# Chunks 1 and 2 of a windowed attention with one softmax group each, and the next projection in front of the down products

## The chip, the cores and the metric

The kernel runs on one core of one Trainium2 chip. The metric is the device time of one execution in microseconds, lower is better. Before the change it was 259.79 us, the median of three runs (259.69 to 259.99).

A core has engines that run side by side, each with its own queue of instructions in order: TensorE (PE in the profile; PEld is its weight load), VectorE (DVE), ScalarE (ACT), GpSimd (POOL) and SyncE (SP), whose queue here only issues DMAs. ACT and POOL issue DMAs too. Semaphores order work between engines.

## What is computed

A layer norm, a windowed attention with 32 heads of 20 elements, in which each position attends to itself and the seven positions 2, 4, ... 14 before it, and a gated bilinear block beside it; both are added to x.

```python
x = A_x                                   # 1 x 2048 x 640
xn = _layernorm(x, axis=-1)
return x + _A_ref(xn, A_wqkv, A_wo) + _B_ref(xn, B_w_gate, B_w_up, B_w_down)
# A: W, dil = 8, 2
logits = jnp.einsum("bhsd,bhswd->bhsw", q, kg) * scale
attn = _softmax(logits, axis=-1)
o = jnp.einsum("bhsw,bhswd->bhsd", attn, vg)      # then o @ wo
# B: F = 1536
g = jnp.einsum("bsd,df->bsf", x, w_gate)
u = jnp.einsum("bsd,df->bsf", x, w_up)
return jnp.einsum("bsf,fd->bsd", g * u, w_down)
```

## The kernel before

The 2048 rows are 16 tiles of 128 (`t`), in four chunks of 512 (`c`, four tiles `q` each). All arithmetic on features works on transposed activations: `xnT` holds the normed rows of a chunk with features on partitions.

For each chunk there are these steps.

- **LN** (`ln`, L344, for chunks 0 and 1 on DVE; `ln_chunk`, L315, for chunks 2 and 3 on ACT: two passes for mean and square, one that applies them). The x tiles are loaded by DMA into five buffers. `LN_HOLD` (L299) names, for each tile of chunks 2 and 3, the step after which its first ACT pass may begin. An entry of two numbers names a hidden block `HT[c, f]`, one of three numbers an eviction of the projection, `R[r, c][j]`.
- **Transposes** (`transposes`, L369): from tile 4 on by transposing DMAs on SP's queue into `xnT`, which has `XB` buffers: two, or three when `EARLY` is set.
- **Projection** (`proj`, L487): 75 matmuls of 512 columns, 25 each for query, key and value, evicted by ACT (L498). `project(c)` also copies the 14 rows of halo for keys and values.
- **Products** (`products` and `fold`, L522 to L567): DVE multiplies the query with the shifted keys of two positions of the window at a time, for one half of the chunk's rows, 2560 elements per instruction, into `pw`, and folds the five feature groups together; the last fold of each pair writes over the first part of the keys' or the queries' buffer.
- **Logits** (`logits`, L569): PE sums those over the 4 partitions of a head with the matrix `Ek` (128 x 32), into `lps`, tag `pl`. Before, each chunk has two groups `g`, one per half of the rows. Each is 8 matmuls of 256 columns in column tiles of 32, four side by side, in one of two `pl` buffers of one PSUM bank.
- **Softmax** (`softmax`, L595), per group: DVE maximum and subtract, ACT exponential (L620), DVE sum, reciprocal and multiply into `a`.
- **Round trip** (`store` and `spread`, L638 to L649): each head's weights are needed on all of its partitions. SP's queue stores `a` (128 KB) to a DRAM tile `aD`, and loads it back with each row repeated on four partitions, as `aE` (512 KB).
- **Value products** (`av`, L661): per tile DVE multiplies the shifted values by `aE`, in two instructions of 2560 elements (L674), and adds the eight window positions in three steps (L684, L682) to `oT`.
- **Gated products** (`glu`, L708): 12 hidden blocks `f`, for each 5 matmuls with `wg` and 5 with `wu` (L717), evicted by ACT to `gs` and `us` (L722) and multiplied by DVE to `hT` (L734).
- **Down** (`down`, L769): per tile and half of the output columns, 12 matmuls with `hT` and `wd` (L783) and 5 with `oT` and `wo` (L786), into one bank, evicted by ACT to `y` (L798). POOL's queue adds `y` to the output by an accumulating DMA (L827), onto x, which was copied there by DMA beforehand (`seed`); the last two tiles are added on DVE and stored by SP. For the first tile of a chunk the ten first hidden blocks and `oT` go first, and the last two blocks follow.

The order in each queue is not written out but planned when the kernel is built. Each step is an `add(engine, cost, fn, deps, occ=...)`; `Plan.order` (L60) walks a model of the engines, takes the step that is ready and whose due time is earliest, and emits the instructions in that order. Due times come from the chain of costs behind a step. `margin` is added in front of a follower, `PACE` scales all costs of an engine, `urgent` puts a step first, and `kb` adds a model of a DMA queue. PE's main work (`pe_main`) is one chain in the order in which the steps are added; the logits are not in this chain and may be put between any two of its steps. So the planned costs move no work by themselves, they decide the order only.

The order of PE's chain is set by the loop at the end (L905 on): attention and gated products of chunk c, LN of chunk c+2, then the four down steps of chunk c, and then the projection of chunk c+2; with `EARLY` the projection comes in front of the down steps.

Of the kernel before, what the change touches and what calls it, by code (L numbers as in the profile page):

```python
# [9 lines left out]
ACT = mybir.ActivationFunctionType  # L10
ALU = mybir.AluOpType
# [21 lines left out]
class Plan:  # L33
# [1 line left out]

    LAG = 0.06
    RAW = 0.116
    PACE = {"DVE": 1.03, "ACT": 1.0}
    INORDER = ("DVE", "PE", "ACT")

    def __init__(self):
# [70 lines left out]
def kernel(  # L112
# [11 lines left out]
    nc = tc.nc  # L124
# [171 lines left out]
    def apply_in(t):  # L296
        XT[t] = inline("DVE", 0.443, ln_apply(t), [RS[t]], 0.4)

    LN_HOLD = ((0,2),(0,3),(0,4),(0,5),(1,2),(1,3),(1,4),(1,5))  # L299

    def held(at):
        return HT[at] if len(at) == 2 else R[at[0], at[1]][at[2]]
# [59 lines left out]
        return main  # L362

    XDMA = 4
    EARLY = False
    XB = 3 if EARLY else 2
    GP = {}

# [58 lines left out]
            X[t + 5] = add("POOL", 6.0, load_x(t + 5, nc.gpsimd), [a], occ=0.45, kb=160)  # L427

    LL = {}
    PV = {}  # L430
    R = {}
    PROJ = ("q", "k", "v")
# [2 lines left out]
    def halo(c, r):  # L435
        def fn():
            k = new((PROJ[r], c), [P, KT, HALO + CS], BF, PROJ[r], 2)
            if c == 0:
                nc.gpsimd.memset(k[:, :, 0:HALO], 0.0)
            else:  # L440
                nc.scalar.copy(k[:, :, 0:HALO], T[PROJ[r], c - 1][:, :, CS : CS + HALO])
        if c == 0:
            HALOCP[r, c] = add("POOL", 0.3, fn, after=[RS[0]])
        else:
            w = LL.get(2 * c - 3) if r == 1 else O16.get(CH * (c - 1) - 1)
            HALOCP[r, c] = add("ACT", 0.25, fn, [w, *R[r, c - 1]])

    def lhs(r, i, j):
# [38 lines left out]
    def proj(c, r, lo=0, n=CS):  # L487
        for j in range(KT):
            key = ("qkv", c, r, j, lo)

            def pe(key=key, j=j):
                new(key, [P, 512], F32, "ps", 6, psum)
                for i in range(KT):
                    nc.tensor.matmul(T[key][:, 0:n], lhsT=lhs(r, i, j),  # L494
                                     rhs=T["xnT", c][:, i, lo : lo + n], start=(i == 0), stop=(i == KT - 1))

            def ev(key=key, j=j):
                nc.scalar.copy(where(r, c, j, j + 1, lo, n)[:, 0, :], T[key][:, 0:n])  # L498

            ts = range(c * CH + lo // P, c * CH + (lo + n) // P)  # L500
            old = LL.get(2 * c - 3) if r < 2 else O16.get(CH * (c - 1) - 1)
            a = pe_main(KT * (n / 2400 + 0.0027), pe, [*WW[r], *[TT[t] for t in ts], *[TX.get(t) for t in ts], old])
            e = add("ACT", 0.16 + n / 1200, ev, [a, HALOCP.get((r, c)), R.get((r, c - 2), [None])[0]], occ=0.07 + n / 1200)
            ring.append(e)
            R.setdefault((r, c), []).append(e)
# [37 lines left out]
    def products(c, hf):  # L543
        for j in range(4):
            i = 4 * hf + j
            u = i // 2

            def mul(u=u, j=j):
                if j % 2 == 0:
                    new(("pw", c, u), [P, 4, KT, HS], BF, *(("av", 2) if c == 0 and hf else ("pw", 2)))  # L550
                o = T["pw", c, u][:, 2 * (j % 2) : 2 * (j % 2) + 2, :, :]
                lo = hf * HS
                qh = T["q", c][:, :, lo : lo + HS]
                kh = T["k", c][:, :, lo + DIL * 2 * j : lo + DIL * 2 * j + HS]
                qh = bass.AP(tensor=qh.tensor, offset=qh.offset, ap=[list(qh.ap[0]), [0, 2], *[list(x) for x in qh.ap[1:]]])
                kh = bass.AP(tensor=kh.tensor, offset=kh.offset, ap=[list(kh.ap[0]), [DIL, 2], *[list(x) for x in kh.ap[1:]]])
                nc.vector.tensor_tensor(o, qh, kh, ALU.mult)  # L557

            m = 8 * c + i
            w = None if c == 0 else LL[0] if c == 1 and hf == 0 and FIRST < 3 else FO[4 * c + u - 2]  # L560
            PW[m] = add("DVE", 1.48, mul, [*R[0, c], *R[1, c], w], occ=1.395, after=[PW.get(m - 1)])
        for u in (2 * hf, 2 * hf + 1):
            FO[4 * c + u] = fold(c, u)

    PAIRED = ()

    E = HS // 4  # L567

    def logits(c, g):  # L569
        n = 2 * c + g  # L570

        def lg():
            l = new(("lps", n), [P, W, E], F32, "pl", 2, psum)
            parts = [summed(c, 2 * g + b) for b in range(2)]
            last = len(parts[0]) - 1
            for i in range(last + 1):
                for b in range(2):
                    for j in range(4):
                        nc.tensor.matmul(l[H * j : H * (j + 1), 4 * b : 4 * b + 4, :], lhsT=Ek[:],  # L579
                                         rhs=parts[b][i][:, :, E * j : E * (j + 1)],  # L580
                                         start=(i == 0 and b == 0), stop=(i == last), tile_position=(0, H * j), skip_group_check=True)

        alone = not (g and c in PAIRED)
        took = 0.022 + 0.2195 * (len(LEFT) if c == 0 else 1) + (0.19 if alone else 0.0)
        LL[n] = add("PE", took + 0.13, lg, [FO[2 * n], FO[2 * n + 1], FO[4 * c + 3] if c in PAIRED else None, LL.get(n - 1), AA.get(n - 2), CE], occ=took)
        LL[n].urgent = True
        LL[n].margin = (0.9 if c == 0 else 2) if alone else 0.0

    def prodlog(c):
        for g in range(2):  # L590
            products(c, g)
        for g in range(2):
            logits(c, g)

    def softmax(c, hf):  # L595
        n = 2 * c + hf

        def small(op, occ, deps):
            return add("DVE", occ + 0.083, op, deps, occ=occ)

        def mask():
            ps = T["lps", n]
            nc.vector.tensor_tensor(ps[0:H, :, 0:HALO], ps[0:H, :, 0:HALO], negm[0:H], ALU.add)

        def top():
            m = new(("m", n), [P, E], F32, "m", 1)
            nc.vector.tensor_reduce(m[:], T["lps", n][:].rearrange("p w s -> p s w"), AX.X, ALU.max)

        def sub():
            d = T["d", n] = T["lps", n]  # L610
            nc.vector.tensor_tensor(d[:], d[:], T["m", n][:, None, :].to_broadcast([P, W, E]), ALU.subtract)

        a = LL[n]
        if n == 0:
            a = small(mask, 0.18, [a, CM])
        a = small(top, 0.6, [a])
        DD[n] = small(sub, 0.609, [a, AA.get(n - 1)])

        def ex():
            nc.scalar.activation(T["d", n][:], T["d", n][:], ACT.Exp, scale=scale)  # L620

        e = add("ACT", 0.635, ex, [DD[n]], occ=0.54)
        e.margin = 0.8

        def total():
            s = new(("s", n), [P, E], F32, "s", 1)
            nc.vector.tensor_reduce(s[:], T["d", n][:].rearrange("p w s -> p s w"), AX.X, ALU.add)

        def rec():
            nc.vector.reciprocal(T["s", n][:], T["s", n][:])  # L630

        def scaled():
            a = new(("a", n), [P, W, E], BF, "a", 1)
            nc.vector.tensor_tensor(a[:], T["d", n][:], T["s", n][:, None, :].to_broadcast([P, W, E]), ALU.mult)

        AA[n] = small(scaled, 0.609, [small(rec, 0.47, [small(total, 0.6, [e])]), AS.get(n - 1)])

        def store():  # L638
            aD = new(("aD", n), [H, 4, W * E], BF, "aD", 2, dram)
            nc.sync.dma_start(out=aD[:].rearrange("h e f -> e h f"), in_=T["a", n][:].rearrange("p w s -> p (w s)"))  # L640

        def spread():
            ae = new(("aE", n), [P, 4, W, E], BF, "aE", 2)
            src = T["aD", n][:]
            src = bass.AP(tensor=src.tensor, offset=src.offset, ap=[[4 * W * E, H], [0, JL], [1, 4 * W * E]])
            nc.sync.dma_start(out=ae[:], in_=src)

        AS[n] = add("SP", 3.3, store, [AA[n], AE.get(n - 2)], occ=0.5, kb=128)
        AE[n] = add("SP", 3.9, spread, [AS[n], AM.get(2 * n - 3)], occ=0.5, kb=512)  # L649

    BY_DMA = ()
    AS = {}
# [6 lines left out]
        WL["o"] = SPLAST[0] = add("SP", 8, wo_load, after=[SPLAST[0]], occ=0.5, kb=800)  # L659

    def av(t):  # L661
        n, u = divmod(t, 2)
        c, q = divmod(t, CH)

        def mul(b):
            def fn():
                if b == 0:
                    new(("av", t), [P, W, KT, P], BF, "av", 2)
                o = T["av", t][:, :, :, b * E : (b + 1) * E]
                w = T["aE", n][:, 2 * u + b, :, :]  # L670
                w = bass.AP(tensor=w.tensor, offset=w.offset, ap=[list(w.ap[0]), [E, W], [0, KT], [1, E]])
                v = T["v", c][:, :, q * P + b * E : q * P + b * E + E]
                v = bass.AP(tensor=v.tensor, offset=v.offset, ap=[list(v.ap[0]), [DIL, W], *[list(x) for x in v.ap[1:]]])
# [10 lines left out]
                    nc.vector.tensor_tensor(v[:, 0:k], v[:, 0:k], v[:, k : 2 * k], ALU.add)  # L684
            return fn

        w = LL[1] if t < 2 else O16.get(t - 2)
        a = add("DVE", 1.48, mul(0), [AE[n], w, *R[2, c]], occ=1.40, after=[O16.get(t - 1) if ONE else AM.get(t - 1)])
        a = AM[t] = add("DVE", 1.48, mul(1), [AE[n]], occ=1.40, after=[a])
        def tree_dma(k):  # L690
            def fn():
                v = T["av", t]
# [193 lines left out]
    def attention(c):  # L886
        prodlog(c)
        if c == 0:
            SPLAST[0] = WL["u"]
            load_down()  # L890
            load_out()
        for hf in range(2):
            softmax(c, hf)
        for q in range(CH):
            av(c * CH + q)

# [58 lines left out]
```

## Time and profile before

| | |
|---|---|
| median of 3 runs | 259.79 us |
| the profiled execution's own time | 258.83 us |
| its span, first to last instruction | 256.9 us |
| PE busy | 251.4 us (98%) |
| DVE busy | 226.2 us (88%) |
| ACT busy | 129.1 us (50%) |
| granted TensorE clock | 0.999 |
| `aE` spread, 512 KB, issue to landing | 3.4 to 4.8 us, median 3.6 |
| `y` store, 160 KB, issue to landing | 3.6 us, median |
| idle time of DVE before value products, for `aE` | 8.9 us in 3 waits |

In the lines of the profile, L is the line of the kernel, the text after it names what is written and read, and xN counts instructions. In the chain of waits in order of time, the columns are start, length and what held the chain; in the timeline, start, length, engine, line and operation, and in brackets how long the engine had been idle and for whom. The matmuls' ends are modelled, so neighbouring matmuls overlap in the timeline by about 0.16 us and the chain counts by ends. The sums by stage give, after the stretch, its length, the busy time and number of instructions of PE, PEld, DVE, ACT and POOL, the granted clock, the share of the DMA engines and their rate.

### The profile page before, as it was taken

The page shows a single profiled execution, that of the slowest core. Times are in us where ns is not written, and L with a number is a line of the kernel's source. Part 1 is how long each engine was busy: PE and PEld are TensorE (multiplying, and loading weights), DVE is VectorE, ACT ScalarE, POOL GpSimd, SP SyncE. Part 2 cuts the span into 40 slices and gives each one's busy share as a digit, 9 for nine tenths or more (in the row PEclk, how much of TensorE's full clock was granted, in tenths as well). Part 3 has the DMA queues.
Part 4 walks back from the last instruction along what each step waited for, and adds up shares of the span by engine and source line. Part 5 has one row for each costly group of instructions (what it writes and reads, how often), then busy time and mean ns, then how long its engine had stood idle before and what let it go on. Part 6 is the DMA issues. An engine that isn't in the chain of part 4 may idle for free.

```text
span 256.9 us, 3821 instructions
## 1 busy us (share of the span) xinstructions
PE 251.4 (98%) x1493; PEld 140.3 (55%) x1493; DVE 226.2 (88%) x299; ACT 129.1 (50%) x251; POOL 33.9 (13%) x59
## 2 busy tenths in 40 slices
PE   6999999999999999999999999999999999999995
PEld 2955554444677555444477655444457654445762
DVE  5679999999999998999999964999999975999911
ACT  2756555798551364689662254655531233754100
POOL 2530000002142100003702110000301210000110
PEclk9999999999999999999999999999999999999999
DMA  7989996102165402032327232020022243020221
GB/s 224 346 200 239 397 374 225 69 23 82 25 117 95 46 12 93 0 102 102 106 52 98 32 46 82 7 97 0 27 79 26 26 61 94 20 82 3 26 26 52
DMA packets 19969, 24.48 MB, mean 95 GB/s; under 512 B 9104, under 2 KB 17296, under 8 KB 19888
## 3 DMA queue, kind: packets, MB, share of 16 engines
q1 hardware_dynamic: 16608, 17.70, 22.2%
q0 software_dynamic: 2384, 5.41, 12.4%
q10 hardware_dynamic: 960, 1.15, 1.3%
q8 instruction: 11, 0.18, 0.3%
q14 instruction: 6, 0.05, 0.1%
HBM read 18.61 MB, written 5.96 MB: 96 GB/s over the span
## 4 chain that ended last, share of the span: by engine, by line
PE 96%; DVE 1%; DMA 1%; ACT 0%; issue 0%
PE ps L717 40%; PE ps L494 23%; PE ps L783 20%; PE ps L786 8%; PE ps L468 2%; PE pl L579 1%; DMA x<-in_A_x_dram 1%; DVE st L252 1%; PE ps L393 0%; ACT xnT L399 0%; DVE x L271 0%; DVE x L794 0%; DVE mv L258 0%; DVE ve L260 0%
## 5 line engine op out<-in xcount | busy, mean ns | idle before, releaser
L717 PE MATMUL ps<-xnT,wu 128*128 128x512 bf16 x240 | 59.7, 379 | 0.0
L717 PE MATMUL ps<-xnT,wg 128*128 128x512 bf16 x240 | 59.6, 379 | 0.0
L783 PE MATMUL ps<-wd,hT 128*128 128x320 bf16 (+2 forms) x384 | 57.4, 299 | 0.0
L674 DVE TENSOR_TENSOR av<-v,aE 128x2560 bf16<-128x2560 bf16 x32 | 47.6, 1486 | 8.9 <-DMA aE<-aD 8.9
L783 PEld LDWEIGHTS <-hT 128*128 128x128 bf16 x384 | 37.0, 98 | 16.1 <-issue 0.4
L557 DVE TENSOR_TENSOR pw<-q,k 128x2560 bf16<-128x2560 bf16 x28 | 40.6, 1486 | 0.9 <-ACT k L498 0.9
L717 PEld LDWEIGHTS <-wg 128*128 128x128 bf16 x240 | 23.5, 98 | 28.1
L717 PEld LDWEIGHTS <-wu 128*128 128x128 bf16 x240 | 23.3, 98 | 28.3 <-issue 0.4
L684 DVE TENSOR_TENSOR av<-av 128x2560 bf16<-128x2560 bf16 (+1 forms) x32 | 36.9, 1154 | 0.3
L722 ACT CAST us<-ps 128x512 bf16<-128x512 f32 x48 | 28.2, 587 | 17.3 <-PE ps L717 17.3
L722 ACT CAST gs<-ps 128x512 bf16<-128x512 f32 x48 | 28.1, 586 | 16.7 <-PE ps L717 16.7
L798 ACT COPY y<-ps 128x320 f32<-128x320 f32 x28 | 11.7, 426 | 45.5 <-PE ps L786 30.7
L786 PE MATMUL ps<-wo,oT 128*128 128x320 bf16 (+2 forms) x160 | 27.0, 299 | 0.0
L528 DVE TENSOR_TENSOR pw<-pw 128x2048 bf16<-128x2048 bf16 (+1 forms) x28 | 25.2, 952 | 0.0
L827 POOL DMA_DIRECT2D out_dram<-y x14 | 12.3, 876 | 82.1 <-ACT y L798 81.6
L494 PE MATMUL ps<-xnT,wk 128*128 128x512 bf16 x100 | 22.6, 380 | 0.0
L734 DVE TENSOR_TENSOR hT<-gs,us 128x512 bf16<-128x512 bf16 x48 | 20.2, 420 | 2.6 <-ACT us L722 2.4
L494 PE MATMUL ps<-xnT,wv 128*128 128x512 bf16 x100 | 22.4, 379 | 0.0
L786 PEld LDWEIGHTS <-oT 128*128 128x128 bf16 x160 | 15.5, 98 | 6.3
L498 ACT CAST k<-ps 128x512 bf16<-128x512 f32 x20 | 11.7, 586 | 11.0 <-PE ps L494 11.0
L494 PEld LDWEIGHTS <-wv 128*128 128x128 bf16 x100 | 11.7, 118 | 9.9 <-issue 0.2
L494 PE MATMUL ps<-xnT,wq 128*128 128x512 bf16 x75 | 16.9, 379 | 0.0
(69 smaller groups left out, 197.0 us busy)
## 6 DMA issues: line engine op xcount, KB each, us to landing
aE<-aD SPq DMA_DIRECT2D x8, 512.0 KB, 3.6
out_dram<-y POOLq DMA_DIRECT2D x14, 160.0 KB, 3.6
out_dram<-in_A_x_dram POOLq DMA_DIRECT2D x3, 640.0 KB, 4.3
wg<-in_B_w_gate_dram SPq DMA_DIRECT2D x1, 1920.0 KB
wu<-in_B_w_up_dram SPq DMA_DIRECT2D x1, 1920.0 KB, 12.7
wd<-in_B_w_down_dram SPq DMA_DIRECT2D x1, 1920.0 KB
x<-in_A_x_dram SPq DMA_DIRECT2D x11, 160.0 KB, 6.4
aD<-a SPq DMA_DIRECT2D x8, 128.0 KB
```

The costliest lines, as they stand in the source:

```text
L494: nc.tensor.matmul(T[key][:, 0:n], lhsT=lhs(r, i, j), rhs=T["xnT", c][:, i, lo : lo + n], start=(i == 0), stop=(i == KT - 1))
L498: nc.scalar.copy(where(r, c, j, j + 1, lo, n)[:, 0, :], T[key][:, 0:n])
L528: nc.vector.tensor_tensor(w[:, :, lo:hi, :], w[:, :, lo:hi, :], w[:, :, a:b, :], ALU.add)
L557: nc.vector.tensor_tensor(o, qh, kh, ALU.mult)
L674: nc.vector.tensor_tensor(o, v, w, ALU.mult)
L684: nc.vector.tensor_tensor(v[:, 0:k], v[:, 0:k], v[:, k : 2 * k], ALU.add)
L717: nc.tensor.matmul(ps[:], lhsT=(wu if r else wg)[:, i, f * P : (f + 1) * P], rhs=T["xnT", c][:, i, :], start=(i == 0), stop=(i == KT - 1))
L722: nc.scalar.copy(s[:], T[key][:])
L734: nc.vector.tensor_tensor(h[:], T["gs", c, f][:], T["us", c, f][:], ALU.mult)
L783: nc.tensor.matmul(ps, lhsT=T["hT", c, f][:, q * P : (q + 1) * P], rhs=wd[:, f, sl], start=(f == 0), stop=(f == FT - 1 and not wo_part))
L786: nc.tensor.matmul(ps, lhsT=T["oT", t][:, g, :], rhs=wo[:, g, sl], start=False, stop=(g == KT - 1 and f1 == FT))
L827: nc.gpsimd.dma_start(out=out_flat[t * P : (t + 1) * P, :], in_=T["y", t][:], accum_op=ALU.add)
```

## The change

Four things are changed together. `GR` gives the number of logits and softmax groups of each chunk: two for chunks 0 and 3, one for chunks 1 and 2. A chunk's groups now share one `pl` tile of two PSUM banks, one `a`, one `aE` (1 MB, one buffer instead of two of 512 KB). In chunks 1 and 2 a group is 8 matmuls of 512 columns, each softmax instruction has twice the elements, one store and one spread carry 256 KB and 1 MB, and a value product is one instruction of 5120 elements per tile. `EARLY` is set, with a third `xnT` buffer. The planned costs of store and spread are 3.6 and 4.2 instead of 3.3 and 3.9, without the model of a queue, `PACE` of DVE is 1.01 instead of 1.03, and `LN_HOLD` lets the LN passes of chunk 2 begin at the projection of chunk 1.

```diff
-    PACE = {"DVE": 1.03, "ACT": 1.0}
+    PACE = {"DVE": 1.01, "ACT": 1.0}
-    LN_HOLD = ((0,2),(0,3),(0,4),(0,5),(1,2),(1,3),(1,4),(1,5))
+    LN_HOLD = ((1,1,0),(2,1,0),(2,1,2),(2,1,4),(0,11),(0,11),(0,11),(0,11))
-    EARLY = False
+    EARLY = True
     XB = 3 if EARLY else 2
+    GR = (2, 1, 1, 2)
...
     def logits(c, g):
-        n = 2 * c + g
+        n = (c, g)
+        E = CS // 4 // GR[c]
         def lg():
-            l = new(("lps", n), [P, W, E], F32, "pl", 2, psum)
-            parts = [summed(c, 2 * g + b) for b in range(2)]
+            if g == 0:
+                new(("lps", c), [P, 2 * CS], F32, "pl", 1, psum)
+            l = T["lps", c][:, g * W * E : (g + 1) * W * E].rearrange("p (w s) -> p w s", w=W)
...
-                        nc.tensor.matmul(l[H * j : H * (j + 1), 4 * b : 4 * b + 4, :], lhsT=Ek[:],
-                                         rhs=parts[b][i][:, :, E * j : E * (j + 1)],
-                                         start=(i == 0 and b == 0), stop=(i == last), tile_position=(0, H * j), skip_group_check=True)
+                        at = g * 4 * E + j * E
+                        rhs = summed(c, 2 * (at // HS) + b)[i][:, :, at % HS : at % HS + E]
+                        first = i == 0 and (b == 0 or GR[c] == 1)
+                        nc.tensor.matmul(l[H * j : H * (j + 1), 4 * b : 4 * b + 4, :], lhsT=Ek[:], rhs=rhs, start=first,
+                                         stop=(i == steps - 1), tile_position=(0, H * j), skip_group_check=True)
-        LL[n].margin = (0.9 if c == 0 else 2) if alone else 0.0
+        LL[n].margin = 0.9 if c == 0 else 1.5
...
-            aD = new(("aD", n), [H, 4, W * E], BF, "aD", 2, dram)
-            nc.sync.dma_start(out=aD[:].rearrange("h e f -> e h f"), in_=T["a", n][:].rearrange("p w s -> p (w s)"))
+            if g == 0:
+                new(("aD", c), [GR[c], H, 4, W * E], BF, f"aD{GR[c]}", 2, dram)
+            nc.sync.dma_start(out=T["aD", c][g].rearrange("h e f -> e h f"), in_=T["a", c][:, g * W * E : (g + 1) * W * E])
...
-            ae = new(("aE", n), [P, 4, W, E], BF, "aE", 2)
-            src = T["aD", n][:]
+            if g == 0:
+                new(("aE", c), [P, 4 * W * P], BF, "aE", 1)
+            src = T["aD", c][g]
...
-        AS[n] = add("SP", 3.3, store, [AA[n], AE.get(n - 2)], occ=0.5, kb=128)
-        AE[n] = add("SP", 3.9, spread, [AS[n], AM.get(2 * n - 3)], occ=0.5, kb=512)
+        AS[n] = add("SP", 3.6, store, [AA[n], AE.get((c - 2, GR[c - 2] - 1))], occ=0.5)
+        AE[n] = add("SP", 4.2, spread, [AS[n], AM.get(CH * c - 1)], occ=0.5)
...
     def av(t):
-        n, u = divmod(t, 2)
         c, q = divmod(t, CH)
+        E = CS // 4 // GR[c]
+        parts = P // E
...
-        a = add("DVE", 1.48, mul(0), [AE[n], w, *R[2, c]], occ=1.40, after=[O16.get(t - 1) if ONE else AM.get(t - 1)])
-        a = AM[t] = add("DVE", 1.48, mul(1), [AE[n]], occ=1.40, after=[a])
+        for b in range(parts):
+            w = 0.065 + 2.67 / parts
+            a = add("DVE", w + 0.085, mul(b), [ae, LL[0, GR[0] - 1] if t < 2 else O16.get(t - 2), *R[2, c]], occ=w,
+                    after=[a or (O16.get(t - 1) if ONE else AM.get(t - 1))])
+        AM[t] = a
```

The softmax's instructions take the slice of their group in the shared tiles `pl`, `m`, `s` and `a`. In the loop at the end nothing else is changed:

```python
        if EARLY and c + 2 < NCH:
            project(c + 2)
        for q in range(CH):
            down(c * CH + q)
        if not EARLY and c + 2 < NCH:
            project(c + 2)
```

## The prediction

> **What bounds the kernel now.** I read the page first (busy time and the chain of waits), then the chain in order of time, then sums by stage, then the queue of SP and the timeline of DVE around the DRAM round trip of the softmax.
>
> ```profile
> span 256.9 us, 3821 instructions
> PE 251.4 (98%) x1493; PEld 140.3 (55%) x1493; DVE 226.2 (88%) x299; ACT 129.1 (50%) x251; POOL 33.9 (13%) x59
> PE 96%; DVE 1%; DMA 1%; ACT 0%; issue 0%
> ```
>
> PE is never let go: the chain is PE from 5.64 us to 253.78 us. So a change gains only what it takes off PE's own stream, and costs what it makes PE wait.
>
> ```profile
> 85.55 2.16 PE ps L494 x10
> 87.71 0.33 PE pl L579 x8
> 88.04 13.08 PE ps L494 x60
> 101.12 0.33 PE pl L579 x8
> 101.45 1.21 PE ps L494 x5
> ...
> 164.12 25.90 PE ps L717 x120
> 190.02 1.36 PE ps L783 x10
> 191.38 0.68 PE ps L786 x5
> 192.06 1.36 PE ps L783 x10
> 193.42 0.68 PE ps L786 x5
> 194.10 2.17 PE ps L783 x16
> ```
>
> Two logits groups (pl) lie in the projection of chunk 2; after the gated products of chunk 2 (to 190.02), down 8 takes its first ten hidden blocks and the attention product, and at 194.10 needs the last two blocks of hT. Stage sums price a group:
>
> ```profile
> 85.55:102.66 17.11, 17.11 (x93) 8.85 (x91) 16.32 (x18) 9.27 (x17) 0.86 (x1) 1.00 0.22 49
> 102.66:128.56 25.90, 25.90 (x123) 11.78 (x121) 25.35 (x33) 19.86 (x41) 7.36 (x7) 1.00 0.23 77
> 128.56:147.47 18.91, 18.91 (x146) 13.36 (x144) 18.56 (x21) 7.36 (x14) 2.69 (x3) 1.00 0.44 62
> 147.47:164.12 16.65, 16.65 (x85) 8.81 (x83) 11.24 (x14) 9.03 (x16) 0.86 (x1) 1.00 0.22 49
> ```
>
> The first number after each stretch is its length; PE and DVE busy are the first and third with a count. The two projections differ by one group: 17.11 - 16.65 = 0.46 us. DVE is as full as PE (16.32 of 17.11, 25.35 of 25.90, 18.56 of 18.91): it is the engine that could become the bound. What it waits for:
>
> ```profile
> 143.17 0.86 POOL L827 DMA_DIRECT2D out_dram<-y  x1 [3.73 <-ACT y L798]
> 148.23 0.86 POOL L827 DMA_DIRECT2D out_dram<-y  x1 [4.20 <-ACT y L798]
> 148.70 0.54 SPq L640 DMA_DIRECT2D aD<-a  x1
> 153.97 0.55 SPq L646 DMA_DIRECT2D aE<-aD  x1
> 157.48 1.49 DVE L674 TENSOR_TENSOR av<-v,aE 128x2560 bf16<-128x2560 bf16 x1 [5.28 <-DMA aE<-aD]
> 165.17 0.55 SPq L640 DMA_DIRECT2D aD<-a  x1
> 168.47 0.54 SPq L646 DMA_DIRECT2D aE<-aD  x1
> 193.01 0.42 DVE L734 TENSOR_TENSOR hT<-gs,us 128x512 bf16<-128x512 bf16 x1
> ```
>
> Store aD to spread aE is 3.3 us at 165.17, but 5.27 where a y store was issued 0.5 us earlier (148.23). DVE lost 5.28 us there, and its last hT of chunk 2 ended at 193.43, half a microsecond ahead of PE's need: DVE's queue was nearly the bound already.
>
> **The change, part by part.**
>
> *Logits, PE.* 120 matmuls of 512 columns take 25.90, so 0.216 each, and 256 columns stream in 0.108. A group streams 2 x 0.108 (four column tiles run side by side); the rest of its cost, 0.44 to 0.46 by stage, is about 0.235 for entering and leaving the form. One group of 512 columns: 0.235 + 2 x 0.216 = 0.667. Before, chunk 1 pays 0.46 + 0.46 and chunk 2 pays 18.91 - 18.47 (down 0, no group) = 0.44, plus 0.46. Saved: 0.92 + 0.90 - 2 x 0.667 = 0.49 us. No row has such a 512-column group: at most it costs what two cost (saves 0), at least what one of 256 does (saves 0.9); the streaming row puts it at 0.49.
>
> *Softmax and value products, DVE.* Each saves fixed time per instruction: 10 softmax instructions and 8 value products fewer. From 2560 and 1280 elements (1.486 and 0.822) an element costs 0.52 ns, so 5120 take 2.82 and hold the queue 2.74, against 2 x 1.40. Like the softmax rows this is off the path as long as DVE meets PE's needs, below.
>
> *Projection c+2 in front of down c; LN of c+2 earlier.* The same matmuls in another order: 0 on PE in itself. What it needs moves with it. ACT's LN passes of chunk 2 (8 statistics passes of 0.93 to 1.03 with their accumulator reads, 4 of 0.92) now lie from the projection of chunk 1 on; ACT is busy 21.1 of the 36 us from 5 to 41, and its order puts them between evictions, so the evictions stay ahead of PE. On POOL three x loads go out before the first y store instead of between y stores; on SP the eight transposes (1.25 us of issue each) go ahead of chunk 1's aD, not around it. With the third xnT buffer they no longer wait for the last gated product. By the same walk as below the last transpose of chunk 2 lands at 62.8, PE wants it at 67.1; chunk 3's at 101.3 for 128.3. So I cost them at nothing; the cover is 4 us of gated products, and if it were gone PE would wait one for one in front of the projection. The two planned costs and PACE change order alone, and that order is what I walk.
>
> *One pl tile, three waits.* Chunk 0's second group now waits for the first group's exponent sums (same tile). In DVE's order one product and two folds stand in front; following DVE's row times the sums end 0.1 us before PE comes. Cost 0; bounds 0 and 0.6, the wait if ACT's exponential (0.59) came one eviction later. The merged groups wait for all four folds instead of two; these end 3 us ahead of PE.
>
> *Round trip.* Between 93.9 and 101.2 us aD moves at a flat 95 GB/s and aE near 400. Doubling adds 131 KB / 95 = 1.38 and 524 KB / 400 = 1.31: aD 3.3 + 1.35 = 4.65, aE 3.6 (page median) + 1.35 = 4.95; with 0.07 of hand-overs R = 9.65 from the end of the scaled attention to the first value product. Bounds: nothing added, 7.0; the whole transfer phases added (1.8 and 2.05, slow starts too), 10.8.
>
> *Does PE then wait?* DVE's order after the change, walked at row pitches. Anchor: hT 1 of chunk 1 waits for ACT; chunk 1's first starts at 105.48 before, the next pair is 2.16 later, minus 0.25 saved by then: 107.39. From there to the start of chunk 2's last hT: 22 hT x 0.335 = 7.4; 18 of 2560 x 1.40 = 25.2; 8 of 5120 x 2.735 = 21.9; 5 of 2048 x 1.135 = 5.7; 12 of 1024 x 0.60 = 7.2; 7 of 1280 x 0.74 = 5.2; 6 oT x 0.40 = 2.4; one double softmax 5.5; top and subtract of chunk 3's first group 1.2; 17 dependent starts x 0.12 = 2.0. Sum 83.8. PE's need is 194.10 - 0.49 + 0.44 (chunk 3's first group now comes before it) less 0.16 of the chain's offset and 0.15 for hand-over and weight load, less the 0.42 of hT and plus 0.14 as it is the second block: 193.45. So DVE may wait 193.45 - 107.39 - 83.8 = 2.26 us in all. It waits twice, R less the work it has between (8.5 in chunk 1 as in chunk 2: folds, three products, hT): 2 x (9.65 - 8.5) = 2.3. That is 0.05 over: the stall in down 8 is 2 x (R - 9.63). Taken 0.1, bounds 0 (R up to 9.6) and 2.3 (R = 10.8). Behind the late hT queue down 8 to 11 and all later PE work; nothing later gives it back.
>
> Sum: 258.83 for the profiled execution (span 256.9 + 1.93 around it) - 0.49 + 0.1 = 258.4. The runs' median is 0.96 above that execution; the same change on it gives 259.4.
>
> **Rivals.**
>
> *A. A y store cuts into the doubled aD of chunk 2 (slower).* The last y store of down 7 follows its stage by 0.76 (147.47, 148.23). After: 128.31 + 16.2 + 19.1 = 163.6, so 164.4, with its packets 1.4 later (as at 148.23) at 165.8. aD of chunk 2 goes out at 162.3 by the same walk and moves packets until about 166.5. For: the trace's collisions cost 5.27 - 3.3 = 2.0 and, at 210.31, 4.82 - 3.6 = 1.2. Against: there the y store came first; here aD does, and the transfer that starts first seems to be served first. It decides from the moment aD is still moving at 165.8. Price 1.2 to 2.0 with no slack left: 259.4 + 1.5 = 260.9. The Trainium skill (DMA: Bandwidth & Descriptors, Queues, rings and completion order) says each engine alternates between queues after whole packets of some 9 to 17 descriptors; by that rule the y store does get in between, or just misses. No row here shows that order.
>
> *B. Transfers slower than their steady rate (slower).* R = 10.8 or part of it: stall up to 2.3, so 260.2 to 261.7. For: aE landings vary from 3.4 to 4.8 at one size. Against: clean aD are all 3.3.
>
> *C. More is gained (faster).* If the unprofiled runs, 0.96 longer than the profile, now hold stalls where the last hT has 0.5 us of cover, the projection in front removes some: 259.4 - 0.6 = 258.8. For: that thin cover. Against: the runs agree within 0.3.
>
> *D. The change does not do what it says:* PE's order, read from the built program, does show the merged groups and the moved projections, so no chance is given.
>
> **How the numbers follow.** Forecast 0.45, A 0.22, B 0.20, C 0.13. What a measurement can tell from no change is 0.2%, 0.52 us, so 259.27 is the border of faster: the forecast lies just inside, and 0.12 of its 0.45 beyond. Faster 0.12 + 0.13 = 0.25; same 0.33 + 0.04 of A + 0.03 of B = 0.40; slower 0.35. Range: from 258.9, inside C, to 261.6, the end of B; the forecast's own is 259.2 to 259.8.
>
> **What would show it.** Right: 8 instead of 16 logits matmuls in chunks 1 and 2 and about 0.67 for each group; DVE waiting 1.0 to 1.3 for aE before both first value products; PE without a gap at down 8. A: an aD of chunk 2 of 6 us and a gap in PE near 194. B: both aE landings above 5.4. The prediction is wrong if PE waits anywhere else, above all at the logits of chunk 0 or 3, or in a projection for xnT.

## The result, and the profile after

The changed kernel takes 261.1 us (median of 12 runs, 260.55 to 264.11) where the kernel before takes 259.92 (median of 12 on the same chip, 259.17 to 260.16). The ratio is 1.0076, 95% interval 1.0056 to 1.0096: slower by 0.8%. The two medians alone are 0.45% apart; the ratio also weighs the four of the 12 runs that lie at 262.8 us or more. The ratios in this document leave out runs more than 1.5% above the fastest of their kernel, two of ten in the two-store kernel and one of six in the last one. Forecast were 259.4 us and no change; 261.1 lies in the stated range, 258.9 to 261.6, near its upper end. The profiled execution took 260.83 us against 258.83.

The page of the changed kernel: instructions and span, busy time, and the shares of the chain of waits.

```profile
span 259.1 us, 3747 instructions
...
PE 250.5 (97%) x1459; PEld 140.2 (54%) x1477; DVE 225.3 (87%) x281; ACT 129.4 (50%) x249; POOL 33.9 (13%) x59
...
PE 48%; DVE 43%; DMA 6%; issue 1%; ACT 1%; SPq 0%; DVEq 0%
```

DVE has a little less work than before (225.3 against 226.2), ACT and POOL nearly the same. PE's 250.5 against 251.4 before is no saving: this profile lacks 18 of PE's 1477 matmuls (the weight loads are all there), and a second profile of the kernel, which has them all, shows 251.4. The chain is no longer PE's: DVE and the round trip hold half of it. The round trip of the two merged groups in SP's timeline (start, length of the issue, line, what it moves):

```profile
106.99 0.54 SPq L662 DMA_DIRECT2D aD<-a  x1
112.82 0.55 SPq L669 DMA_DIRECT2D aE<-aD  x1
...
164.25 0.54 SPq L662 DMA_DIRECT2D aD<-a  x1
170.13 0.54 SPq L669 DMA_DIRECT2D aE<-aD  x1
```

A spread is issued when its store has landed, so the stores took 5.83 and 5.88 us, where the prediction had 4.65. The first value product of each chunk, in DVE's timeline, with its idle time and what it waited for in brackets:

```profile
118.61 2.83 DVE L698 TENSOR_TENSOR av<-v,aE 128x5120 bf16<-128x5120 bf16 x1 [2.97 <-DMA aE<-aD]
...
175.10 2.83 DVE L698 TENSOR_TENSOR av<-v,aE 128x5120 bf16<-128x5120 bf16 x1 [2.28 <-DMA aE<-aD]
```

From the end of the scaled attention (106.98 and 164.22 in the chain) to these starts the trip R is 11.63 and 10.88 us, and DVE waited 2.97 + 2.28 = 5.25 us. Where PE pays for it, in PE's timeline:

```profile
166.08 0.29 PE L586 MATMUL pl<-k,Ek 128*32 128x256 bf16 x4 [0.28 <-DVE k L534]
166.68 0.29 PE L586 MATMUL pl<-q,Ek 128*32 128x256 bf16 x4 [0.30 <-DVE q L534]
...
194.05 0.84 PE L816 MATMUL ps<-wo,oT 128*128 128x320 bf16 x5
194.73 0.30 PE L813 MATMUL ps<-wd,hT 128*128 128x320 bf16 x1
197.14 2.08 PE L813 MATMUL ps<-wd,hT 128*128 128x320 bf16 x14 [2.11 <-DVE hT L764]
```

In down 8 the eleventh hidden block is there and the twelfth is not: 2.41 us between two starts that lie 0.14 apart otherwise, so 2.27 lost. The first group of chunk 3 waits for two late folds: it takes 1.26 us out of the stream (from the start of the matmul before to the start of the one behind, less that matmul's 0.216), where the same group takes 0.43 in the wide-store kernel below, which does not wait: 0.84 lost. A merged group lengthens the stream around it by 0.65 and 0.66: the 17 matmuls of half a tile take 2.96 and 2.97 us with the group among them (96.32 to 99.28 and 150.60 to 153.57), 2.31 without. Before, the pairs cost 0.47 + 0.47 and 0.43 + 0.46, counted in the same way: 0.52 gained. 2.27 + 0.84 - 0.52 = 2.6, and PE's last matmul starts 2.64 us later than before (256.17 and 253.53). The final store landed about 0.4 sooner, so the span grew by 2.2.

### The profile page after: what moved, and what is told of

Its sections match the earlier page's. It is cut to its first block, busy times and chain, and to the rows that moved or that the text cites. A ratio compares the mean times of both kernels' runs of the same rounds, so it can differ in the third digit from the quotient of the medians.

```text
span 259.1 us, 3747 instructions
## 1 busy us (share of the span) xinstructions
PE 250.5 (97%) x1459; PEld 140.2 (54%) x1477; DVE 225.3 (87%) x281; ACT 129.4 (50%) x249; POOL 33.9 (13%) x59
## 4 chain that ended last, share of the span: by engine, by line
PE 48%; DVE 43%; DMA 6%; issue 1%; ACT 1%; SPq 0%; DVEq 0%
PE ps L747 22%; DVE av L698 11%; PE ps L495 10%; PE ps L813 9%; DVE pw L558 8%; DVE av L708 8%; DVE pw L529 6%; PE ps L816 4%; DVE hT L764 3%; PE ps L469 2%; DMA aD<-a 2%; DMA aE<-aD 2%; DVE oT L706 2%; DMA x<-in_A_x_dram 1%; DVE k L534 1%
## 5 line engine op out<-in xcount | busy, mean ns | idle before, releaser
L698 DVE TENSOR_TENSOR av<-v,aE 128x2560 bf16<-128x2560 bf16 (+1 forms) x24 | 46.2, 1932 | 6.5 <-DMA aE<-aD 6.4
L495 PEld LDWEIGHTS <-wk 128*128 128x128 bf16 x100 | 11.7, 117 | 9.6
```

Of the source, the lines that this page charges most:

```text
L495: nc.tensor.matmul(T[key][:, 0:n], lhsT=lhs(r, i, j), rhs=T["xnT", c][:, i, lo : lo + n], start=(i == 0), stop=(i == KT - 1))
L698: nc.vector.tensor_tensor(o, v, w, ALU.mult)
```

## The experiments

**Is it the new order or the merged groups?** The changed kernel with two groups in every chunk:

```diff
-    GR = (2, 1, 1, 2)
+    GR = (2, 2, 2, 2)
```

> The changed kernel with two groups in every chunk again (GR = 2, 2, 2, 2): only the order of projection and down, the LN start and the planned costs remain of the change. Theory T (the round trip of the merged groups took 11.6 and 10.9 us from the end of the scaled attention to the first value product, not 9.65, and makes DVE late for the last hT of chunk 2 and for the folds of chunk 3): store 3.3 and spread 3.5 to 4.0 as before, no wait of PE after 14 us, the logits' 0.5 us is not saved, so 259.9, ratio 0.998 to 1.002. Rival U (the new order itself, with LN and transposes moved, costs PE): 260.9 or more, with PE waiting in the projections or in down.

Measured 258.75 us (12 runs), ratio 0.997 (0.9953 to 0.9988). PE has no wait in the stream, its share of the chain is 98%. So the rest of the change is faster than the kernel before, not slower and not equal: the projection in front, LN's earlier start, the planned costs and the shared tiles, which no run takes apart. The whole loss, 2.35 us between the medians of 261.1 and 258.75 and what the merging saves, comes with the merged groups. The two medians were taken on two occasions; against the kernel before, the ratios are 1.0076 and 0.997.

The other half, the merged groups in the old order (the new planned costs stay):

```diff
-    LN_HOLD = ((1,1,0),(2,1,0),(2,1,2),(2,1,4),(0,11),(0,11),(0,11),(0,11))
+    LN_HOLD = ((0,2),(0,3),(0,4),(0,5),(1,2),(1,3),(1,4),(1,5))
-    EARLY = True
+    EARLY = False
```

> The changed kernel with EARLY off, two xnT buffers and the old LN_HOLD: merged groups in the old order. Theory T: the merged round trips still take 10.5 to 11.6, DVE is late for hT in down 4 or down 8, PE waits 0.5 to 2 us; 260.3 to 261.6. Rival U: without the new order nothing waits and the saving of the logits is left, 259.4.

Measured 260.06 us, ratio 1.0023 (0.9999 to 1.0047), no clear difference from the kernel before and a little under the expected 260.3. The stores take the same 5.83 and 5.9 us, and PE waits once more for hT in down 8, but less. The waits view (engine, what waited, for what; sum, times, longest):

```profile
PE ps L813 <- DVE hT L764: 0.8, 1, 0.8
```

The slow trip belongs to the merged groups in either order.

**Where did this gain come from?** The kernel before, profiled again:

> The kernel before, profiled a second time. Its first profiled execution took 258.83 us, less than every one of its 12 runs (259.17 to 260.16). Theory C (the usual execution holds stalls of PE that the first profile did not catch, in a down stage where the last hT had 0.5 us of cover): an execution of 259.4 to 260.2 shows gaps in PE's stream of 0.3 to 1.2 us in all, at the last hidden blocks of down 8 or down 4 or at a logits group, behind a store or spread of more than 3.6 us. Rival (the 0.9 us lies outside the span, or in the start): no such gaps, and the span longer only before 14 us or not at all.

> The kernel before, profiled once more, to see where its usual executions (median 259.7 to 259.9) are longer than the profiled one (258.83, no wait of PE). Theory C: PE waits at the last hT of chunk 3 (in down 12), 0.3 to 1.0 us, and the execution is longer than 258.83 by about that wait. Rival: no wait of PE above 0.1 us after the first 10 us, and the execution is as long as the first, or longer by something spread over the whole span.

> As before_look2: a third profile of the kernel before. Theory C: a wait of PE of 0.3 to 1.0 us in down 12 wherever the execution is above 259.1; rival: none.

These executions took 259.29, 259.49 and 259.70 us, all longer than the 258.83 of the profile that the prediction was made from. In each of them PE waits in down 12. The page of the second has this line of shares of its chain of waits, and the chain in order of time (start, length, what held it) these pieces:

```profile
PE 59%; DVE 31%; DMA 8%; issue 1%; ACT 0%; SPq 0%
```
```profile
142.91 0.70 DVE m L607
...
148.79 5.32 DMA aD<-a
154.13 3.61 DMA aE<-aD
157.76 1.49 DVE av L674
...
238.07 1.40 DVE av L674
239.86 2.21 PE ps L783 x15
```

From the softmax of chunk 2 (142.91) to down 12 the chain is DVE and the round trip, not PE: the last hT of chunk 3 comes late. Between the two starts at PE's wait lie 0.50, 0.58 and 0.48 us in the three executions, 0.14 without a wait: 0.34 to 0.44 lost, of the 0.45, 0.55 and 0.89 us by which PE's last matmul starts later than in the first profile. In that first profile the hT came just in time, and the chain read "PE 96%". The rest of the excess lies in the start: the last 35 query matmuls of chunk 0 start at 11.21, 11.23 and 11.66 us where they started at 11.13, so 0.08, 0.10 and 0.53 later. Wait and start together give 0.44, 0.54 and 0.87 of the 0.45, 0.55 and 0.89. The two-group version has no wait in down 12. That accounts for about 0.4 of the 0.95 us between the medians of the kernel before (259.7 in this comparison) and of that version; the rest was not located.

**Does the slow trip have to cost anything?** The changed kernel, with only the planner's costs of the merged groups set to what the trip takes; the same instructions in another order:

```diff
-        AS[n] = add("SP", 3.6, store, [AA[n], AE.get((c - 2, GR[c - 2] - 1))], occ=0.5)
-        AE[n] = add("SP", 4.2, spread, [AS[n], AM.get(CH * c - 1)], occ=0.5)
+        AS[n] = add("SP", 5.9 if GR[c] == 1 else 3.6, store, [AA[n], AE.get((c - 2, GR[c - 2] - 1))], occ=0.5)
+        AE[n] = add("SP", 5.4 if GR[c] == 1 else 4.2, spread, [AS[n], AM.get(CH * c - 1)], occ=0.5)
```

> The changed kernel; for the merged groups alone the planned costs are what the trace measured, store 5.9 and spread 5.4 instead of 3.6 and 4.2, so only the order of DVE (and ACT) changes. Theory T: other work of DVE fills the trip, the last hT of chunk 2 comes in time, PE does not wait; 0.5 saved in the logits, 259.4, ratio 0.997 to 0.999. Rival W (DVE has too much work in that stage whatever its order): the stall stays, 260.8 to 261.3.

Measured 258.28 us, ratio 0.995 (0.9933 to 0.9966). SP's timeline:

```profile
159.23 0.54 SPq L662 DMA_DIRECT2D aD<-a  x1
165.28 0.54 SPq L669 DMA_DIRECT2D aE<-aD  x1
```

The store still takes 6.05 us, but in chunk 2 it is issued at 159.23 instead of 164.25; PE loses about 0.45 us in all around 194. With the order made for the trip's true length the median is 0.47 us under the two-group version's, about what the merged logits save, though the two intervals overlap. The expected 259.4 left out what the rest of the change gains.

**Why is the store slow?** In the changed kernel the DMA view of the stretch 106.9 to 113.0, in 40 equal slices of 0.15 us, shows what the store moves; below it the store of half the size in the kernel before, 165.1 to 168.6, slices of 0.09 us.

```profile
GB/s 0 0 0 0 0 0 0 0 40 54 54 13 0 13 27 0 13 0 54 67 54 81 40 94 107 94 107 94 94 107 107 107 107 67 81 27 13 0 0 0
DMA packets 132, 0.26 MB, mean 43 GB/s; under 512 B 4, under 2 KB 4, under 8 KB 132
```
```profile
GB/s 0 0 0 0 0 0 0 0 0 0 0 0 0 0 47 47 23 35 23 35 82 82 82 94 94 94 94 94 94 94 105 94 94 82 12 0 0 0 0 0
DMA packets 132, 0.13 MB, mean 37 GB/s; under 512 B 4, under 2 KB 132, under 8 KB 132
```

Both have 128 data packets, of 2048 and 1024 bytes, and come near 100 GB/s in the end. The first starts with ten slices (1.5 us) in which 33 KB move, the second with six (0.5 us) for 18 KB. At 95 GB/s these bytes take 0.34 and 0.19, so the start costs 1.2 us instead of 0.3: 0.85 of the 1.18 us that were missing in the prediction's store; the other 0.33 were not located. The first ten slices look the same in both stores of the merged groups in the old order. Two kernels change the store alone or with the spread. In the first, the store goes out as two of 128 KB:

```diff
-            nc.sync.dma_start(out=T["aD", c][g].rearrange("h e f -> e h f"), in_=T["a", c][:, g * W * E : (g + 1) * W * E])
+            for k in range(3 - GR[c]):
+                lo, hi = k * W * E // (3 - GR[c]), (k + 1) * W * E // (3 - GR[c])
+                nc.sync.dma_start(out=T["aD", c][g].rearrange("h e f -> e h f")[:, :, lo:hi], in_=T["a", c][:, g * W * E + lo : g * W * E + hi])
```

> The changed kernel; each store of 256 KB is two of 128 KB, of 1024 B per row instead of 2048 B, one behind the other on SP's queue; spread as it was. Theory D (the store of the merged group takes 5.8 and not 4.65 because the first rows of a 2048 B transfer come slowly; bytes and engines are the same): both halves landed 4.6 to 5.0 after the first is issued, R about 10, PE waits under 1 us, 259.5 to 260.3. Rival (it is the bytes over 4 engines, whatever their rows): 5.6 to 6.0 again, and 260.8 to 261.3.

The pair takes 4.82 and 4.81 us from the first issue to the spread's issue, near the 4.65 that the prediction had for one store, and the first store starts as the small one did: 16 KB in 0.6 us. Yet the median of the ten runs is 261.53 us, ratio 1.0042 (1.001 to 1.0074): still slower than the kernel before, and not clearly better than the changed kernel, whose interval overlaps. The expected 259.5 to 260.3 was missed; single runs go from 259.27 to 268.45. In the profiled execution (262.95 us) the spread took the gain back, as the DMA view shows for chunk 2's spread in this kernel and in the changed one (packets, MB and share of q0, POOL's queue, and issue to landing of the spread in the last column):

```profile
q0 software_dynamic: 73, 0.07, 8.4%
...
aE<-aD SPq DMA_DIRECT2D x1, 1024.0 KB, 6.9
```
```profile
q0 software_dynamic: 16, 0.02, 1.9%
...
aE<-aD SPq DMA_DIRECT2D x1, 1024.0 KB, 5.0
```

More of a y store lies inside the spread of this kernel, which was issued earlier; that this made it longer is not shown. From the store's issue to the first value product the two trips take 10.47 and 11.77 us, 22.24 together; in the changed kernel 22.47. DVE waits 5.02 us for them, 5.25 there.

In the second, `aD` is laid out so that the store goes from 128 partitions to 128 rows, and each tile's quarter of the spread is a transfer of its own:

```diff
+            d = T["aD", c][g]
+            o = d.rearrange("h e f -> e h f") if GR[c] == 2 else d.rearrange("h e f -> (h e) f")
+            nc.sync.dma_start(out=o, in_=T["a", c][:, g * W * E : (g + 1) * W * E])
...
+            wide = GR[c] == 1
+            for e in range(4 if wide else 1):
+                n4 = W * E if wide else 4 * W * E
+                lo = g * 4 * W * E + e * n4
+                part = bass.AP(tensor=src.tensor, offset=src.offset + e * H * n4, ap=[[n4, H], [0, JL], [1, n4]])
+                nc.sync.dma_start(out=T["aE", c][:, lo : lo + n4], in_=part)
```

> The changed kernel; in the merged groups the DRAM tile is laid out in the order of a's partitions, so that the 256 KB store is 128 rows in one dimension and not 4 x 32 and should go over 16 DMA engines instead of 4, and the spread is four transfers of 256 KB, one per tile, so that a value product waits for its own quarter. Theory T: store 2.5 to 3.3, first quarter some 3 after it, R about 6; DVE waits less than 0.6 at these products, PE does not wait; 259.4. Rival W: 260.8 to 261.3.

Measured 258.14 us, ratio 0.994 (0.9919 to 0.9961). DMA view of this store, 107 to 110, slices of 0.075 us:

```profile
GB/s 0 0 0 0 0 0 0 0 0 0 0 0 191 355 355 328 382 382 382 410 410 246 55 0 0 0 0 0 0 0 0 0 0 0 0 0 0 0 0 0
DMA packets 144, 0.26 MB, mean 87 GB/s; under 512 B 16, under 2 KB 16, under 8 KB 144
...
aD<-a SPq DMA_DIRECT2D x1, 256.0 KB, 2.0
```

The same 128 packets of 2048 bytes have no slow start here and run at four times the rate: 2.04 us (2.94 in chunk 2, where a y store of 144 packets runs beside it). The count of small packets tells on how many engines a transfer runs, 4 before and 16 now. The Trainium skill (DMA: Bandwidth & Descriptors, Why a DMA increments its semaphore by 16 and not by 1) states the rule: the engines used are the largest number up to 16 that divides the slowest dimension of both sides, and each posts one count at the end; 4 x 32 rows against 128 partitions gives 4, 128 rows give 16. The trace agrees. It says nothing of the slow start, whose cause stays open. The rows also lie side by side in DRAM now, where they were 8 KB apart, and this run does not separate that from the number of engines. The two-store kernel kept the 8 KB and had the shorter start, so the spacing alone is not the cause.

What the split spread is worth by itself, with the old store:

```diff
-            src = bass.AP(tensor=src.tensor, offset=src.offset, ap=[[4 * W * E, H], [0, JL], [1, 4 * W * E]])
-            nc.sync.dma_start(out=T["aE", c][:, g * 4 * W * E : (g + 1) * 4 * W * E], in_=src)
+            k = 4 if GR[c] == 1 else 1
+            for e in range(k):
+                n4 = 4 * W * E // k
+                lo = g * 4 * W * E + e * n4
+                part = bass.AP(tensor=src.tensor, offset=src.offset + e * n4, ap=[[4 * W * E, H], [0, JL], [1, n4]])
+                nc.sync.dma_start(out=T["aE", c][:, lo : lo + n4], in_=part)
```

> The changed kernel; the spread of 1 MB is four of 256 KB, one per tile, so a value product waits for its own quarter; the store of 256 KB goes over 4 engines as it did. Theory T: store 5.8, first quarter 3 to 3.5 behind it, R about 9.2; DVE waits 0.5 to 0.8 at the first product, PE does not wait; 258.2 to 258.7. Rival (the store alone decides): 260 or more.

Measured 258.3 us, ratio 0.9948 (0.9931 to 0.9964). DVE's timeline, the first value products:

```profile
116.94 2.83 DVE L702 TENSOR_TENSOR av<-v,aE 128x5120 bf16<-128x5120 bf16 x1 [0.94 <-DMA aE<-aD]
...
172.27 2.83 DVE L702 TENSOR_TENSOR av<-v,aE 128x5120 bf16<-128x5120 bf16 x1 [1.12 <-DMA aE<-aD]
```

The stores still take 5.87 and 6.0 us, but the first product needs a quarter of the spread only: 2.06 us of waiting in place of 5.25, below the 2.26 that the prediction allowed, and PE has no wait. That agrees with the allowance. It also shows that the faster store is not needed for the time of the wide-store version.

**The changed kernel once more**, to see that its profile is no accident:

> The changed kernel, profiled a second time. Theory (slow 2048 B stores): both stores of the merged groups take 5.7 to 6.0 us from issue to the issue of the spread, and PE waits 1.5 to 2.7 us for the second last hT of chunk 2 in down 8, 260.2 to 261.4 in all. Rival (an accident of one execution): one of the stores takes 4.6 to 5.0, and the wait is below 1 us.

260.82 us. The stores take 5.84 and 5.85 us, and 2.38 us lie between the two starts in down 8: the same picture.

**Does a wait of PE cost more than itself?** Four of the changed kernel's 12 runs are at 262.8 to 264.1 us with a mean granted clock of 0.993, the other eight at 260.6 to 261.3 and 1.000. The two-store kernel was profiled in such an execution (262.95 us, 0.993). Its sums by stretch (length, busy time of PE, PEld, DVE, ACT and POOL with counts, then the granted clock):

```profile
194.40:197.20 2.80, 0.29 (x4) 0.02 (x2) 2.80 (x3) 0.00 (x0) 0.00 (x0) 1.00 0.01 2
197.20:198.00 0.80, 0.80 (x5) 0.49 (x6) 0.80 (x2) 0.47 (x2) 0.00 (x0) 0.69 0.00 0
198.00:199.00 1.00, 1.00 (x5) 0.56 (x4) 0.96 (x2) 0.36 (x1) 0.34 (x1) 0.50 0.06 16
...
200.00:201.00 1.00, 1.00 (x6) 0.56 (x4) 0.96 (x3) 0.00 (x0) 0.00 (x0) 0.54 0.96 81
201.00:202.00 1.00, 1.00 (x10) 0.70 (x9) 0.97 (x2) 0.21 (x1) 0.00 (x0) 1.00 0.70 83
```

Behind the wait the clock falls to half for some 3.4 us (0.5 + 2.0 + 0.9 in these stretches). To see whether that follows the wait, chunk 2's store is made later in the changed kernel, by storing half of it twice:

```diff
-            nc.sync.dma_start(out=T["aD", c][g].rearrange("h e f -> e h f"), in_=T["a", c][:, g * W * E : (g + 1) * W * E])
+            for hi in (W * E // 2, W * E)[c != 2 :]: nc.sync.dma_start(out=T["aD", c][g].rearrange("h e f -> e h f")[:, :, :hi], in_=T["a", c][:, g * W * E : g * W * E + hi])
```

> The changed kernel with half of chunk 2's weights stored once more in front of its own store, so that the first value product of chunk 2 comes later and PE waits longer in down 8; the same instructions on all engines otherwise. Part of the changed kernel's runs lie near 263 at a granted clock of 0.993 where most lie near 260.9 at 1.000, and in the two-store kernel's profile the clock falls to 0.5 for some 3.5 us right behind a wait of 2.5 us. Theory (a wait that is long enough costs twice: the wait, and half clock for some 3.5 us behind it, 1.7 us more): the wait grows by what the extra store adds, 1.5 to 5.5 us, to 3.6 to 7.6; behind it the granted clock is near 0.5 for 3 to 4 us in the profile, the mean clock is 0.993 in every run, and the time is 260.8 plus the growth plus 1.7: 264.0 to 268.0. Rival (the lower clock has nothing to do with the wait): time grows by the growth of the wait alone, 262.3 to 266.3, and the clock is 0.993 in about one run of three as before.

Measured 265.52 us (4 runs, 264.75 to 266.25), ratio 1.0219 (1.0196 to 1.0242). That lies in both expected ranges, so the profile of an execution of 266.25 us has to tell. PE's timeline at the end of down 8's first tile:

```profile
193.99 0.31 PE L813 MATMUL ps<-wd,hT 128*128 128x320 bf16 x1 [1.96 <-DVE hT L764]
194.72 0.31 PE L813 MATMUL ps<-wd,hT 128*128 128x320 bf16 x1 [0.43 <-DVE hT L764]
...
200.39 3.84 PE L813 MATMUL ps<-wd,hT 128*128 128x320 bf16 x15 [2.51 <-DVE hT L764]
```

The growth came as three waits instead of one, 5.4 us in all against 2.27. Behind the longest, 15 matmuls take 3.84 us, 2.21 in the changed kernel's chain: 1.6 us more, again at half clock (0.50 in the sums from 201 to 204). The mean clock was lower in three of the four runs (0.994, 0.994, 0.985), and 1.000 in one: the expectation's "in every run" fails. None of the 29 runs of the kernel before in the first experiments' comparison shows such a clock, and none of the 34 of the two-group, longer-plan, wide-store and split-spread versions; of the merged groups in the old order, whose wait is 0.8 us in the profile, one in 12 does. So this lower clock goes with a wait, but not in each execution. Half clock for 3.4 us of 261 lowers the mean by 0.0065, so by this estimate the changed kernel's four runs at 0.993 hold one such stretch each; that it lay behind their wait in down 8 was not profiled.

**The best of these**, the wide-store version with one group in chunk 3 too:

```diff
-    GR = (2, 1, 1, 2)
+    GR = (2, 1, 1, 1)
```

> The kernel of wide_store with chunk 3 merged too (GR = 2, 1, 1, 1). If PE's stream is all that is left there: one logits group less, 0.2 us, so 257.9 against 258.14. Rival (chunk 3's round trip, with nothing but glu behind it to fill DVE, makes down 12 late): 258.5 or more, PE waiting near 236.

Measured 257.74 us, ratio 0.9924 (0.9912 to 0.9936), faster than both kernels. PE has no wait in the stream of the profiled execution. One of the six runs took 333.44 us at a mean clock of 0.756, and one of the two-store kernel 268.45 at 0.948. Neither was profiled, and a stretch of 3.4 us is far too short for them, so a low clock has another cause too.

## Why the prediction was wrong

**The size of the trip: the step that failed.** "R = 9.65" was a sum of two terms sized by the steady rate, "aD 3.3 + 1.35 = 4.65, aE 3.6 + 1.35 = 4.95". The store took 5.83 and 5.88, for the most part because its first packets are slower at this size; the spread 5.79 and 4.97. So 2.41 us of the 3.2 that were missing in the two trips are the stores', and nearly all of the rest is one spread's, in which no other queue moved a packet; why it was slow is open. R was 11.63 and 10.88, both above the upper bound of 10.8, which had the right idea ("slow starts too") but took the start of the smaller store for it. That clean stores were "all 3.3" was named as evidence against; they were all of one size, and say nothing of another.

**The place and the formula: right.** The wait came at the last hT of chunk 2 in down 8. "2 x (R - 9.63)" is, with both trips as measured, 11.63 + 10.88 - 19.26 = 3.25 us; PE lost 2.27 there and 0.84 in front of it, 3.11. The walk of DVE's queue held: from the hT at 107.41 to the last hT of chunk 2 at 196.75, less 5.25 of waiting, are 84.1 us where it had 83.8. The split spread agrees with the allowed wait. Two small slips change little: the terms of the walk add to 83.7, not 83.8, and those of R to 9.67, not 9.65, so that the forecast stall would be nothing instead of 0.1.

**The cover of chunk 3's folds: not priced.** The prediction looked at the merged groups' folds, which did end in time, and named the logits of chunk 3 only as a place that would prove it wrong. DVE's delay reached them first, and 0.84 us was lost there; it is no addition to the formula, since it makes PE's need for the hT later by the same.

**"So I cost them at nothing": wrong, on the other side.** The change without the merging gained 0.3% in the two-group version. What bounds the kernel was read from an execution in which PE was "never let go"; three others had PE waiting in down 12. That is rival C's mechanism, at chunk 3 rather than chunk 2, and it was present; the merged trips outweighed it. That 261.1 lies inside the range is in part luck: without a stall the median would be 259.79 - 0.49 = 259.3, and with the 3.11 that PE lost 262.4, outside it; the gain of 0.95 us, which the forecast did not have, took the time back under 261.6.

**The logits and the value products: right.** The four groups before took 1.83 us (1.82 in the prediction), the two merged ones 1.31 (1.33): 0.52 saved for 0.49. A value product of 5120 elements takes 2.83 us, for 2.82.

**The pl tile, LN and the transposes: right.** Chunk 0's groups wait for nothing, before and after, and PE waits for no xnT behind the first 14 us.

**The rivals.** A, the y store in chunk 2's aD, is not the cause: chunk 1's store, with no y store near it, took as long (5.83 and 5.88). The Trainium skill's rule that an engine alternates between queues (DMA: Bandwidth & Descriptors, Queues, rings and completion order) lets a y store in; one did run inside chunk 2's store, which took 0.05 us longer than chunk 1's. B is what happened in the time, and R went past its bound; of its sign, both spreads above 5.4, only one came (5.79 and 4.97), for the excess was more in the stores. Its chance of 0.20 was too low: a price with no row at its size deserved more than a fifth for the upper end.

## What to carry to other kernels

A transfer twice as large is not the old time plus bytes at the steady rate: look at how a transfer of that size starts and on how many engines it runs, and if no row shows it, let the slow end carry real chance. Before calling an engine the bound, look at more than one execution: a hidden block that comes just in time in one is a wait in the next. When a long wait is suspected, first give the planner the true length of the trip, or split the transfer so that the first consumer needs a part of it; both took nearly the whole loss away here without making the store faster.

## What the hardware showed that was not expected

- Stores of 128 packets over 4 engines: 1024-byte packets start with 0.5 us at 35 GB/s, 2048-byte packets with 1.5 us at 21 GB/s; over 16 engines, and with the rows side by side in DRAM, the latter have no slow start (2.04 us in all against 5.83). Why is not known.
- The 1 MB spread took 5.0 to 5.8 us with at most 17 packets of POOL's queue inside it; with 73 of them 6.9 (two stores), with 161 of them 7.6 (longer plan). That they are the reason was not tested.
- A wait of PE of 2.5 us can halve its clock for some 3.4 us behind it, 1.6 us on top. The Trainium skill (TensorE: Matmul & The Clock Gate, Part 1) puts the idle window after which the clock drops at about 3.4 us, free-running. The length of the slow stretch agrees with that figure. The wait does not: 2.8 us between two matmul starts were enough in two profiles, while 2.4 were not in two others.
